# A mixture-of-experts kernel: the 64-row tile of experts 2 to 7 takes the last slots and is worked on behind a test

## The chip, the cores and the metric

The kernel runs on one core of a Trainium2 chip. A core has TensorE (PE in the profile, its weight loads PEld), VectorE (DVE), ScalarE (ACT), GpSimd (POOL) and SyncE (SP), each with its own stream of instructions; a "q" behind a name (PEldq, ACTq) is that engine's sequencer, which handles waits, register loads and branches itself. The metric is the time of one execution in microseconds, the median over runs.

## The reference

A linear attention (a complex-valued decay, 4 batches, 8 heads, 768 steps) gives x with 3072 tokens of 384 numbers. What the change touches is the mixture of experts behind it:

```python
logits = x @ w_gate                                   # 8 experts
noisy_logits = logits + np.log1p(np.exp(x @ w_noise)) * noise
top2 = np.argpartition(-noisy_logits, 2, axis=1)[:, :2]
top2_w = ...                                          # softmax over the two
for e in range(8):
    for k in range(2):
        mask = top2[:, k] == e
        h = np.maximum(x[mask] @ w1[e], 0.0)          # w1[e]: 384 x 1024
        out[mask] += top2_w[mask, k, None] * (h @ w2[e])   # w2[e]: 1024 x 384
```

Each token goes to two of eight experts, so an expert has 768 tokens on average; how many it has is known only when the gates have been computed.

## The kernel before

**Slots.** While the attention runs, each token's row is scattered to a slot of its two experts in a table `xs` in memory. `base_run` counts up by expert: in the end it holds 3072·e plus the tokens of expert e. An expert has room for `CAP` = 832 slots; the slots from `FILL` = 640 on are filled first with empty rows whose token number is out of bounds, so gathers and scatters skip them. If an expert has more than 832 or fewer than 640 tokens (or the decays are extreme), a flag sends the program through a slow path at the end (L856 to L861); in the profiled execution that path is jumped over.

**Tiles.** An expert's 832 slots are worked on in two windows: window 0 has slots 0 to 319 (tiles 0, 1 of 128 rows and tile 2 of 64), window 1 has slots 320 to 831 (tiles 3 to 6). `load_x` brings the rows into `xga` and `xgb`; `x_T` transposes them on PE into `px`, ACT casts them to the high part `x[:, 0]`, DVE subtracts for the low part `x[:, 1]`. `mm1` is the first product, 72 matmuls per window of 320 or 512 columns into `ph`; ACT and DVE make `h` of it. `mm2` is the second product by tile: 24 matmuls of 384 columns for a 128-row tile (L569), 16 for the 64-row tile (L574, L577). DVE multiplies by the gate and adds to the rows `ao[j]` gathered before (`gather_o`, L556), and POOL scatters them to the output (L583). For the 64-row tile ACT copies half of `po` first (L580), and DVE adds twice (L581, L582).

**Order.** Products are made of fp32 numbers split into a high and a low part, which is why each product stands three times. `po` and `px` have two buffers each, `ph` has four. A scheduler puts the instructions of the experts' part in order by priority; the loop over experts writes them as `mm1(e, 0)`, `mm1(e, 1)`, `mm2(e, 0)`, `x_T(e+1, 0)`, `mm2(e, 1)`, `x_T(e+1, 1)`. Weights of the next expert come through three buffers `raw` and are split by ACT (L490) and DVE (L491).

Of the kernel before, what the change touches and what calls it, by code (L numbers as in the profile page):

```python
# [13 lines left out]
I32 = mybir.dt.int32  # L14
AF = mybir.ActivationFunctionType
OP = mybir.AluOpType
# [61 lines left out]
def kernel(  # L78
# [8 lines left out]
    nc = tc.nc  # L87
# [5 lines left out]
    E = w_gate.shape[1]  # L93
# [17 lines left out]
    cp = ctx.enter_context(tc.tile_pool(name="cp", bufs=1))  # L111
# [30 lines left out]
    base_run = cp.tile([128, E], F32, name="base_run")  # L142
# [303 lines left out]

    x3 = xs.rearrange("(e i) r -> e i r", e=E)
    TW = [128, 128, 64, 128, 128, 128, 128]

    def load_x(e, w, dst):  # L450
        if w == 0:
            nc.sync.dma_start(dst[:, 0:2], x3[e, 0:256].rearrange("(p j) r -> p j r", j=2))
            nc.sync.dma_start(dst[0:64, 2], x3[e, 256:320])
        else:
            nc.sync.dma_start(dst, x3[e, 320:CAP].rearrange("(p j) r -> p j r", j=4))

# [11 lines left out]
    def mt(shape, dt, name, **kw):  # L470

        return where.setdefault(name, mpools[-1]).tile(shape, dt, name=name, **kw)
# [38 lines left out]
    def x_T(e, w):  # L511
# [11 lines left out]
        for kk in range(KD):  # L523
            x = XW[w, kk] = mt([128, 2, n], F32R, name=f"x{w}{kk}")
            p = ps_tile("px")
            for j in js:
                o = 128 * (j - js[0])
                gz = nc.tensor.transpose(p[:, o:o + TW[j]], src_t[0:TW[j], j - js[0], kk * 128:(kk + 1) * 128],  # L528
                                    ident[0:TW[j], 0:TW[j]])
                if (e, w) == (0, 1):  # L530
# [22 lines left out]
    def gather_o(e):  # L553
        for j in range(7):
            w = TW[j]
            nc.gpsimd.indirect_dma_start(  # L556
                out=ao[j][0:w, :], out_offset=None, in_=out,
                in_offset=bass.IndirectOffsetOnAxis(ap=OX[e][0:w, j:j + 1], axis=0),
                bounds_check=N - 1, oob_is_err=False)

    def mm2(e, w):
        for j in JS[w]:
            n, o = TW[j], 128 * (j - JS[w][0])
            p = psO.tile([128, 512], F32, name="po")
            a, g = ao[j][0:n, :], GW[e][0:n, j:j + 1]
            if n == 128:
                ms = [(f, i, k2) for f in range(KF) for i, k2 in ((0, 0), (0, 1), (1, 0))]
                for m, (f, i, k2) in enumerate(ms):
                    nc.tensor.matmul(p[:, :DM], HT[w, f][i][:, o:o + 128], W2[f // 2][k2][:, f % 2, :],  # L569
                                     start=(m == 0), stop=(m == len(ms) - 1))  # L570
            else:

                for f in range(KF):
                    nc.tensor.matmul(p[0:2 * n, :DM], HT[w, f][0][:, o:o + 2 * n], W2[f // 2][0][:, f % 2, :],  # L574
                                     start=(f == 0), stop=(f == KF - 1), skip_group_check=True)
                for f in range(KF):
                    nc.tensor.matmul(p[0:n, :DM], HT[w, f][0][:, o:o + n], W2[f // 2][1][:, f % 2, :],  # L577
                                     start=False, stop=(f == KF - 1), skip_group_check=True)
                lo = mt([n, DM], F32, name="lo")
                nc.scalar.copy(lo, p[n:2 * n, :DM])  # L580
                nc.vector.scalar_tensor_tensor(a, lo, g, a, op0=OP.mult, op1=OP.add)  # L581
            nc.vector.scalar_tensor_tensor(a, p[0:n, :DM], g, a, op0=OP.mult, op1=OP.add)  # L582
            nc.gpsimd.indirect_dma_start(  # L583
                out=out, out_offset=bass.IndirectOffsetOnAxis(ap=OX[e][0:n, j:j + 1], axis=0),
                in_=a, in_offset=None, bounds_check=N - 1, oob_is_err=False)
# [34 lines left out]
    for g in range(NG):  # L620
        for lo, hi in ((0, B),) if g < NG - 2 else ((0, B - 1), (B - 1, B)):
            at(B * g + hi + .5 + P["gl"], glog, g, lo, hi)
            at(B * g + hi + .5 + P["gd"], gdis, g, lo, hi)
        if g == NG - 4:
            at(B * g + hi + .5 + P["gd"], load_x, 0, 0, xga)
# [20 lines left out]
    at(NT - .5 - P["q"] + .01, open_pool, qctx)  # L646
    at(P["xt"] + .5, x_T, 0, 0)
    at(P["xt"] + .51, load_x, 1, 0, xga)
    at(P["xu1"] + .5, x_T, 1, 0)
    at(P["w1b"] + .5, load_w1, 1)  # L650
# [30 lines left out]
    for a in ao:  # L681
        nc.vector.memset(a, 0.0)
    load_x(0, 1, xgb)
    mm2(0, 0)
    mm1(1, 0)
    x_T(0, 1)
    load_x(2, 0, xga)
    mm1(0, 1)
    load_x(1, 1, xgb)
    load_w1(2)  # L690
    mm2(0, 1)
    x_T(1, 1)

    lim = mp.tile([128, E], F32, name="lim")
# [3 lines left out]
    nc.vector.tensor_scalar(decm, decm, DEC_MIN, None, op0=OP.is_lt)  # L700
    nc.vector.tensor_reduce(bad[0:112, 0, 1:2], decm[0:112], axis=AX.X, op=OP.max)
    nc.vector.tensor_scalar(bad[:, 1], bad[:, 1], TAN_MAX ** 2, None, op0=OP.is_gt)
    few = mp.tile([128, E], F32, name="few")
    nc.vector.scalar_tensor_tensor(few, lim, float(FILL - CAP), base_run, op0=OP.add, op1=OP.is_gt)
    nc.vector.tensor_tensor(lim, base_run, lim, op=OP.is_gt)
# [14 lines left out]
    for e in range(1, E):  # L720
        load_w2(e)
        gather_o(e)
        if e > 1:
            mm1(e, 0)
            if e + 1 < E:
                load_x(e + 1, 0, xga)
        mm1(e, 1)
        if e + 1 < E:
            load_x(e + 1, 1, xgb)
            if e > 1:  # L730
                load_w1(e + 1)
        mm2(e, 0)
        if e + 1 < E:
            x_T(e + 1, 0)
        mm2(e, 1)
        if e + 1 < E:
            x_T(e + 1, 1)
# [169 lines left out]
```

## Time and profile before

| | |
|---|---|
| median of 3 runs | 731.22 us (730.6 to 732.15) |
| the profiled execution | 730.95 us, of which the span from first to last instruction 729.3 us |
| PE matmul / weight load | 687.4 us (94% of the span) / 609.9 us (84%) |
| DVE / ACT / POOL | 417.6 us (57%) / 329.2 us (45%) / 169.1 us (23%) |
| granted PE clock, mean | 0.992 |

The attention takes about the first 270 us; the rest is the experts, one about every 58 us, with PE hardly ever idle. Busy PE time counts overlapping matmuls as they are modelled, so times between starts are the better measure: eight matmuls of `po` start within 1.39 us.

### The profile page before, as it was taken

Reading aid. Unit: us, or ns where it says so; the run is one execution under the profiler, and the core shown is the slowest. Engines: PE = TensorE matmul, PEld = TensorE weight load, DVE = VectorE, ACT = ScalarE, POOL = GpSimd, SP = SyncE. Lnnn points to the kernel's source line nnn. Section 1 sums busy time; section 2 is a strip of 40 time slices with the busy share of each in tenths; the row PEclk is TensorE's granted clock in tenths of the full one; section 3 lists DMA queues with packets and bytes.
Section 4 is the critical chain, followed back from the end, with each engine's and each line's share of the span. In section 5 each row is a group of like instructions: output and inputs, shape, how many; then the busy total and the mean of one; then the engine's idle time right before and its main releaser. Section 6 shows DMA issues by size and latency. Waiting matters only on the chain.

```text
span 729.3 us, 13448 instructions
## 1 busy us (share of the span) xinstructions
PE 687.4 (94%) x5184; PEld 609.9 (84%) x5184; DVE 417.6 (57%) x946; ACT 329.2 (45%) x545; POOL 169.1 (23%) x187
## 2 busy tenths in 40 slices
PE   1689999999999989999999999999999999999995
PEld 0377687978788979898998998999999899899895
DVE  6788899999988575454264245236227227325321
ACT  6689989897854542423043124124115205203300
POOL 2000002233311263023224124124023123223211
PEclk9989999999999999999999999999999999999998
DMA  7477776844372566145154136028028126212101
GB/s 265 109 246 228 240 211 208 238 140 135 104 221 83 171 208 221 51 133 169 66 191 123 55 123 199 23 88 271 11 66 273 31 74 230 72 37 71 43 28 39
DMA packets 64090, 100.18 MB, mean 137 GB/s; under 512 B 26290, under 2 KB 46363, under 8 KB 64016
## 3 DMA queue, kind: packets, MB, share of 16 engines
q1 hardware_dynamic: 54464, 71.68, 31.9%
q0 software_dynamic: 9552, 27.54, 10.8%
q8 instruction: 43, 0.70, 0.4%
q14 instruction: 31, 0.25, 0.1%
HBM read 68.55 MB, written 32.08 MB: 138 GB/s over the span
## 4 chain that ended last, share of the span: by engine, by line
PE 76%; DVE 9%; ACT 6%; DMA 4%; issue 2%; SPq 1%; POOL 0%; POOLq 0%; DVEq 0%; ACTq 0%
PE ph L545 28%; PE po L569 27%; PE ptr L298 3%; PE psc L307 3%; PE px L528 2%; PE cum L251 2%; DMA raw<-in_moe_w_dram 2%; PE cum L275 2%; PE po L574 2%; PE po L577 2%; PE pY L356 1%; PE psc L545 1%; ACT tr L200 1%; ACT t L200 1%; PE pY L354 1%
## 5 line engine op out<-in xcount | busy, mean ns | idle before, releaser
L569 PE MATMUL po<-w2h,h 128*128 128x384 f32 x768 | 198.8, 336 | 0.0
L545 PE MATMUL ph<-x,w1h 128*128 128x512 f32 (+1 forms) x720 | 194.8, 355 | 0.7 <-DVE h L550 0.5
L545 PEld LDWEIGHTS ph<-x,w1h 128*128 128x128 f32 x720 | 127.8, 188 | 17.0 <-ACT h L547 0.7
L569 PEld LDWEIGHTS po<-w2h,h 128*128 128x128 f32 x768 | 138.9, 188 | 0.9
L569 PE MATMUL po<-w2l,h 128*128 128x384 f32 x384 | 129.0, 336 | 0.0
L545 PE MATMUL ph<-x,w1l 128*128 128x512 f32 (+1 forms) x360 | 127.5, 355 | 0.0
L550 DVE SCALAR_TENSOR_TENSOR h<-ph,h 128x512 fp32r<-128x512 f32 (+2 forms) x176 | 73.3, 453 | 85.3 <-ACT h L547 85.1
L583 POOL DMA_INDIRECT out_dram<-ao,ox x56 | 54.6, 975 | 286.7 <-DVE ao L582 258.0
L547 ACT ACTIVATE h<-ph 128x512 fp32r<-128x512 f32 (+1 forms) x120 | 61.0, 523 | 115.1 <-PE ph L545 100.4
L582 DVE SCALAR_TENSOR_TENSOR ao<-po,gw,ao 128x384 f32<-128x384 f32 (+1 forms) x56 | 34.2, 612 | 121.0 <-PE po L569 120.9
L421 POOL DMA_INDIRECT xs<-xr,sl x48 | 53.8, 1121 | 207.9 <-ACT t L200 103.3
L545 PEld LDWEIGHTS ph<-x,w1l 128*128 128x128 f32 x360 | 67.6, 188 | 7.9
L569 PEld LDWEIGHTS po<-w2l,h 128*128 128x128 f32 x384 | 72.1, 188 | 0.7
L490 ACT CAST w2h<-raw 128x768 fp32r<-128x768 f32 x32 | 26.7, 837 | 91.2 <-PE po L569 87.1
L556 POOL DMA_INDIRECT ao<-out_dram,ox x49 | 54.6, 1113 | 46.2 <-DMA out_dram<-ao,ox 33.4
L307 PE MATMUL psc<-qT,kT 112*128 112x128 f32 x384 | 52.6, 282 | 0.0
L307 PEld LDWEIGHTS psc<-qT,kT 112*128 112x128 f32 x384 | 48.5, 197 | 2.7 <-issue 1.2
L356 PE MATMUL pY<-am,v 128*48 128x128 f32 x384 | 41.4, 275 | 1.2 <-DVE am L308 1.2
L491 DVE TENSOR_TENSOR w2l<-raw,w2h 128x768 fp32r<-128x768 f32 x32 | 30.7, 958 | 13.6 <-ACT w2h L490 12.4
L298 PE MATMUL ptr<-ident,qh 128*112 128x128 f32 x192 | 29.3, 284 | 8.6 <-ACT kT L299 7.9
L580 ACT COPY lo<-po 64x384 f32<-64x384 f32 x8 | 3.8, 477 | 73.4 <-PE po L577 73.3
L491 DVE TENSOR_TENSOR w1l<-raw,w1h 128x1024 fp32r<-128x1024 f32 x24 | 29.2, 1222 | 12.5 <-ACT w1h L490 12.4
(209 smaller groups left out, 981.6 us busy)
## 6 DMA issues: line engine op xcount, KB each, us to landing
raw<-in_moe_w_dram SPq DMA_DIRECT2D x24, 512.0 KB
raw<-in_moe_w_dram SPq DMA_DIRECT2D x32, 384.0 KB
qk<-in_qk_dram SPq DMA_DIRECT2D x24, 384.0 KB
xgb<-xs SPq DMA_DIRECT2D x8, 800.0 KB
re<-in_a_dram SPq DMA_DIRECT2D x12, 384.0 KB
im<-in_a_dram SPq DMA_DIRECT2D x12, 384.0 KB
v<-in_v_dram SPq DMA_DIRECT2D x24, 192.0 KB
out_dram<-zero SPq DMA_DIRECT2D x12, 384.0 KB
```

Of the source, the lines that this page charges most:

```text
L298: nc.tensor.transpose(p[:, h, :], x[:, h, :, :].rearrange("p r x -> p (r x)")[:, 0:112], ident)
L307: nc.tensor.matmul(p[:, j, :], KT[n][:, h, :], QT[n][:, h, :], start=True, stop=True)
L356: nc.tensor.matmul(o, V[n][:, h, :], AM[n][:, h, :], start=not g, stop=True, skip_group_check=True)
L421: d = nc.gpsimd.indirect_dma_start(out=xs, out_offset=bass.IndirectOffsetOnAxis(ap=sl[:, kk, b:b + 1], axis=0), in_=XR[g][:, lo + b, :], i ...
L491: d = nc.vector.tensor_tensor(lo, raw_t, hi.bitcast(F32), op=OP.subtract)
L545: LAST['m'] = nc.tensor.matmul(p[:, :n], W1[e, kk][i][:, f * 128:(f + 1) * 128], XW[w, kk][:, j, :], start=(m == 0), stop=(m == len(ms) - 1))
L547: nc.scalar.activation(h[:, 0:n], p[:, :n], AF.Relu)
L550: LAST['h'] = nc.vector.scalar_tensor_tensor(h[:, dst:dst + b - a], p[:, a:b], 0.0, h[:, a:b].bitcast(F32), op0=OP.max, op1=OP.subtract)
L556: nc.gpsimd.indirect_dma_start(out=ao[j][0:w, :], out_offset=None, in_=out, in_offset=bass.IndirectOffsetOnAxis(ap=OX[e][0:w, j:j + 1], ax ...
L569: nc.tensor.matmul(p[:, :DM], HT[w, f][i][:, o:o + 128], W2[f // 2][k2][:, f % 2, :], start=(m == 0), stop=(m == len(ms) - 1))
L582: nc.vector.scalar_tensor_tensor(a, p[0:n, :DM], g, a, op0=OP.mult, op1=OP.add)
L583: nc.gpsimd.indirect_dma_start(out=out, out_offset=bass.IndirectOffsetOnAxis(ap=OX[e][0:n, j:j + 1], axis=0), in_=a, in_offset=None, bound ...
```

## The change

For experts 2 to 7 tile 2 now holds slots 768 to 831, and window 1 holds slots 256 to 767; experts 0 and 1 keep the old layout. DVE computes `tail`, eight numbers that are 1 where the expert has more than 768 tokens. In `mm2`, tile 2 of experts 2 to 7 stands in an `If`: PE, DVE, ACT and POOL each load the expert's number into a register, compare it and branch. The first product, the gather of `ao[2]` and the transposes of tile 2 are made in any case.

```diff
+    TAILS = range(2, E)
     def load_x(e, w, dst):
         if w == 0:
             nc.sync.dma_start(dst[:, 0:2], x3[e, 0:256].rearrange("(p j) r -> p j r", j=2))
-            nc.sync.dma_start(dst[0:64, 2], x3[e, 256:320])
+            t = CAP - 64 if e in TAILS else 256
+            nc.sync.dma_start(dst[0:64, 2], x3[e, t:t + 64])
         else:
-            nc.sync.dma_start(dst, x3[e, 320:CAP].rearrange("(p j) r -> p j r", j=4))
+            o = 256 if e in TAILS else 320
+            nc.sync.dma_start(dst, x3[e, o:o + 512].rearrange("(p j) r -> p j r", j=4))
...
+    def tail_value(e, engines):
+        return nc.values_load(tail[0:1, e:e + 1], engines=engines, min_val=0, max_val=1,
+                              skip_runtime_bounds_check_because="the result of a comparison")
+
     def mm2(e, w):
         for j in JS[w]:
+            if TW[j] < 128 and e in TAILS:
+                more = tail_value(e, (ENG.PE, ENG.DVE, ENG.Activation, ENG.Pool))
+                with tc.If(more > 0):
+                    mm2_tile(e, w, (j,))
+            else:
+                mm2_tile(e, w, (j,))
+
+    def mm2_tile(e, w, js):
+        for j in js:
...
+    tail = cp.tile([1, E], I32, name="tail")
+    nc.vector.scalar_tensor_tensor(tail, lim[0:1], -64.0, base_run[0:1], op0=OP.add, op1=OP.is_lt)
```

An `If` is scheduled as one piece, and that moves other work. On PE, behind the second tile of expert 2 (the names: `po` second product, `px` transposes of expert 3's rows, `ph` expert 3's first product), there stood before:

```order
L569 MATMUL po<-w2h_4602,h_4725 128x384
L574 MATMUL po<-w2h_4584,h_4627 128x384 [waits DVE_49]
...
L577 MATMUL po<-w2l_4603,h_4725 64x384
L528 MATMUL px<-ident,xga 128x128 [waits DMAHW2_49,PE_49]
...
L569 MATMUL po<-w2h_4584,h_4741 128x384 [waits DVE_49,Activation_49]
...
L528 MATMUL px<-ident,xga 128x128 [waits DVE_49]
```

and now there stands:

```order
L586 MATMUL po<-w2h_4604,h_4727 128x384
L532 MATMUL px<-ident,xga 128x128 [waits DMAHW2_49,PE_49]
...
L549 MATMUL ph<-x_4959,w1h_4850 128x320 [waits DVE_49,Activation_49]
...
L532 MATMUL px<-ident,xgb 128x128 [waits DMAHW7_49,DVE_49]
...
L566 TENSOR_LOAD tail [waits DVE_49]
L573 COMPARE_AND_BRANCH
L591 MATMUL po<-w2h_4586,h_4629 128x384
...
L594 MATMUL po<-w2l_4605,h_4727 64x384
L573 UNCONDITIONAL_BRANCH
L573 UNCONDITIONAL_BRANCH [waits PE_49]
L586 MATMUL po<-w2h_4586,h_4743 128x384
```

Ahead of the branch now stand 16 transposes (9 of window 0, 7 of the 12 of window 1) and 8 matmuls of the next expert's first product; before, six transposes followed tile 2 directly, three stood among the matmuls of tile 3, and the 12 of window 1 came after tile 6. The 16 matmuls of tile 2 lie between the two branches. Who skips them lands on the second unconditional branch, at which PE waits for its own count (`PE_49`), that is until every matmul ahead of it has ended.

On DVE, at the same place (`ao` sums of the tiles, `x` the low parts of expert 3's rows), there stood first:

```order
L582 SCALAR_TENSOR_TENSOR ao_3658<-po,gw,ao_3658 128x384 [waits DMASW6_49,PE_49]
L581 SCALAR_TENSOR_TENSOR ao_3659<-lo,gw,ao_3659 64x384 [waits DMASW7_49,Activation_49]
L533 TENSOR_TENSOR x_4950<-px,x_4950 128x320 [waits Activation_49]
L582 SCALAR_TENSOR_TENSOR ao_3659<-po,gw,ao_3659 64x384 [waits DVE_49]
L533 TENSOR_TENSOR x_4957<-px,x_4957 128x320 [waits Activation_49]
L533 TENSOR_TENSOR x_4964<-px,x_4964 128x320 [waits Activation_49]
L582 SCALAR_TENSOR_TENSOR ao_3660<-po,gw,ao_3660 128x384 [waits DMASW0_49,PE_49]
```

and now:

```order
L599 SCALAR_TENSOR_TENSOR ao_3658<-po,gw,ao_3658 128x384 [waits DMASW6_49,PE_49]
L537 TENSOR_TENSOR x_4959<-px,x_4959 128x320 [waits Activation_49]
...
L537 TENSOR_TENSOR x_5098<-px,x_5098 128x512 [waits Activation_49]
L566 TENSOR_LOAD tail [waits DVE_49]
L573 COMPARE_AND_BRANCH
L598 SCALAR_TENSOR_TENSOR ao_3659<-lo,gw,ao_3659 64x384 [waits DMASW7_49,Activation_49]
L599 SCALAR_TENSOR_TENSOR ao_3659<-po,gw,ao_3659 64x384 [waits DVE_49,PE_49]
L573 UNCONDITIONAL_BRANCH
L573 UNCONDITIONAL_BRANCH [waits DVE_49]
L599 SCALAR_TENSOR_TENSOR ao_3660<-po,gw,ao_3660 128x384 [waits DMASW0_49,PE_49]
```

All four `x` differences that PE waits for now stand ahead of DVE's branch. For expert 7, which has no next expert, PE's branch follows the second tile directly:

```order
L586 MATMUL po<-w2h_7294,h_7417 128x384
L566 TENSOR_LOAD tail
L573 COMPARE_AND_BRANCH
L591 MATMUL po<-w2h_7276,h_7319 128x384 [waits DVE_49]
...
L594 MATMUL po<-w2l_7295,h_7417 64x384
L573 UNCONDITIONAL_BRANCH
L573 UNCONDITIONAL_BRANCH [waits PE_49]
L586 MATMUL po<-w2h_7276,h_7431 128x384 [waits DVE_49,Activation_49]
```

There the first matmul of tile 3 also waits for DVE, which has to empty the buffer of tile 1.

## Rows read from the trace of the kernel before

**Rows 1.** Chain that ended last, share by line (the page's part 4).

```profile
PE 76%; DVE 9%; ACT 6%; DMA 4%; issue 2%; SPq 1%; POOL 0%; POOLq 0%; DVEq 0%; ACTq 0%
```

**Rows 2.** Stretches: us, busy of PE, PEld, DVE, ACT, POOL, clock, DMA share, GB/s.

```profile
413.38:472.08 58.70, 58.23 (x327) 53.81 (x325) 24.79 (x49) 17.26 (x30) 15.57 (x14) 1.00 0.36 117
472.08:530.47 58.39, 58.39 (x327) 53.88 (x325) 24.88 (x49) 17.41 (x30) 14.68 (x14) 1.00 0.36 119
```

**Rows 3.** Whom PE waited for from 354.98 to 704.96 us.

```profile
PE ph L545 <- DVE h L550: 0.5, 1, 0.5
```

**Rows 4.** The chain in order of time: start us, us, what.

```profile
469.30 1.39 PE po L574 x8
470.69 1.39 PE po L577 x8
472.08 0.99 PE px L528 x6
...
702.19 1.39 PE po L574 x8
703.58 1.39 PE po L577 x8
```

**Rows 5.** POOL's DMA queue, experts 2 to 7 in turn: packets, MB, share.

```profile
q0 software_dynamic: 864, 2.38, 12.3%
q0 software_dynamic: 864, 2.33, 11.4%
q0 software_dynamic: 864, 2.47, 11.8%
q0 software_dynamic: 864, 2.34, 12.2%
q0 software_dynamic: 864, 2.32, 12.5%
q0 software_dynamic: 864, 2.25, 12.3%
```

**Rows 6.** Line 856, PE's register load: ns min/median/max, start us.

```profile
L856 PEldq TENSOR_LOAD <-flag x1: 496/496/496, 718.3 to 718.3; - x1
```

**Rows 7.** Instructions of each engine from 718.34 us to PE's end.

```profile
718.34:721.70 3.36, 3.27 (x19) 2.95 (x17) 0.05 (x1) 0.00 (x0) 0.97 (x1) 1.00 0.15 52
```

**Rows 8.** Line 858, the branch over the slow path, by engine.

```profile
L858 ACTq COMPARE_BRANCH  x1: 50/50/50, 705.9 to 705.9; - x1
L858 ACTq EVENT_SEMAPHORE  x1: 17/17/17, 708.4 to 708.4; - x1
L858 PEldq COMPARE_BRANCH  x1: 3617/3617/3617, 719.4 to 719.4; - x1
L858 PEldq EVENT_SEMAPHORE  x1: 51/51/51, 723.0 to 723.0; - x1
L858 POOLq COMPARE_BRANCH  x1: 45/45/45, 723.2 to 723.2; - x1
```

**Rows 9.** Line 903, POOL's next instruction behind that branch.

```profile
L903 POOLq DRAIN  x3: 45/107/4671, 723.7 to 729.0; - x3
```

**Rows 10.** DMA of instruction blocks for PE from 719.4 to 723.1 us.

```profile
q8 instruction: 1, 0.02, 1.5%
```

**Rows 11.** Timeline around one tile 2: start us, us, engine, line, what.

```profile
410.27 0.33 PE L569 MATMUL po<-w2h,h 128*128 128x384 f32 x1
410.64 0.62 DVE L582 SCALAR_TENSOR_TENSOR ao<-po,gw,ao 128x384 f32<-128x384 f32 x1 [3.54 <-PE po L569]
...
414.10 0.27 PE L528 MATMUL px<-ident,xga 64*128 64x64 f32 x1
414.30 0.19 PEld L569 LDWEIGHTS po<-w2h,h 128*128 128x128 f32 x1
...
415.63 0.58 PE L528 MATMUL px<-ident,xga 128*128 128x128 f32 x3
416.25 0.43 ACT L532 CAST x<-px 128x320 fp32r<-128x320 f32 x1 [1.41 <-PE px L528]
416.71 0.49 DVE L533 TENSOR_TENSOR x<-px,x 128x320 fp32r<-128x320 f32 x1 [0.85 <-ACT x L532]
```

**Rows 12.** The chain where expert 3's first product waits for weights.

```profile
431.68 5.80 DMA raw<-in_moe_w_dram
437.50 1.06 ACT w1h L490
438.58 1.23 DVE w1l L491
```

More of the change, by code (lines that the diff above doesn't have):

```diff
@@ L448 @@
     TW = [128, 128, 64, 128, 128, 128, 128]
+    TAILS = range(2, E)
+    ENG = mybir.EngineType
     def load_x(e, w, dst):
```

## The prediction

> **What bounds the kernel now.** I began with the chain that ended last: 76% of it is PE, and no other engine has a tenth [rows 1]. A share is an average, so I then cut the experts' part into periods of one expert. In two of them PE is busy 58.23 of 58.70 us and 58.39 of 58.39 us, at a granted clock of 1.00, that is 2.4 GHz, while DVE, ACT and POOL have 25, 17 and 15 us, and DMA a share of 0.36 [rows 2]. The list of waits says the same: over 350 us PE waited once for another engine, for 0.5 us [rows 3]. The reader should see that here a matmul less is its time less, and that work taken from another engine is worth nothing by itself. The chain in order of time gives the price of what can be skipped: the two halves of tile 2 take 1.39 us each, with transposes right behind them [rows 4], so 2.78 us per expert.
>
> **Who skips.** The profile doesn't print the token counts, but POOL's DMA queue moves each token's row of 384 fp32 numbers (1536 bytes) twice per expert, gathered and scattered, and leaves empty slots out. 768 tokens would be 2 x 768 x 1536 bytes = 2.36 MB. Experts 2 to 7 moved 2.38, 2.33, 2.47, 2.34, 2.32 and 2.25 MB [rows 5], or about 775, 758, 804, 762, 755 and 732 tokens. So experts 2 and 4 run tile 2, and 3, 5, 6 and 7 skip it: gross 4 x 2.78 = 11.1 us of PE. The copy, two sums and scatter that ACT, DVE and POOL skip lie beside PE's 58 us: nothing.
>
> **Load and compare.** A register load on PE's sequencer took 0.496 us [rows 6] and a compare where nothing was far away 0.045 to 0.05 us [rows 8]. Six experts pay 0.55 us each if PE's array stands still meanwhile, 3.3 us in all; nothing if the sequencer is ahead. It is ahead: when it began that load at 718.3 us, the array still had 19 matmuls and 17 weight loads before it [rows 7]. The order shows 24 matmuls between tile 1 and the load (16 transposes, 8 of the first product), so the 17 nearest, at 0.165 us or a little less (six transposes in 0.99 us [rows 4]), keep the array busy for some 2.5 us, and the load ends about 2 us before the array runs dry. That cover is gone only if the sequencer itself is held by a wait shortly before the load; the last that could are transposes waiting for DVE to free `px`. I take 0 (bounds 0 and 0.55), also for experts 2 and 4. On DVE, ACT and POOL the same instructions delay only sums, casts and scatters that PE needs microseconds later.
>
> **The bubble of a skip.** Who skips lands on a jump that waits for PE's own count, so the array must drain. From the start of the last transpose: 0.27 its own time, 0.04 until a semaphore is seen (410.27 + 0.33 to 410.64), 0.19 for the next weights [rows 11]; 0.05 for the waiting instruction; and about 0.20 for the jump, since POOL went from its compare at 723.2 to the DRAIN at 723.7 through two jumps in some 0.45 us [rows 8, 9]. Sum 0.75, less the 0.165 that a next matmul would have come later anyway: 0.59. Experts 3, 5 and 6 thus save 2.78 - 0.59 = 2.2 us each (bounds of the bubble 0.3, without jump and wait, and 0.9: savings 2.5 to 1.9).
>
> Expert 7 has nothing between tile 1 and the branch, and tile 3 needs the `po` buffer of tile 1, which tile 2 used to give DVE time to empty. Now: 0.33 last matmul, 0.04, 0.62 DVE's sum, 0.04, 0.05, 0.19 = 1.27, less 0.17 = 1.10 (the jump passes beside the sum). It saves 1.7 us (bounds 1.5 to 1.9).
>
> **Work that moves.** Transposes and 8 first-product matmuls of the next expert now stand ahead of the branch, and tile 3 behind it. PE has the same work in another order, so it costs only where it waits. A transposed tile goes through ACT and DVE: from three transposes starting at 415.63 to DVE's end at 417.20, 1.57 us [rows 11]. Three such tiles follow each other through two `px` buffers, with window 1's transposes and the 8 matmuls to fill in; laying these rows end to end I get 0.1 to 0.2 us of waiting, about as much as the old order lost around its own transposes (58.70 less 58.23 in one period, 0 in the next [rows 2]). I take 0; five boundaries at 0.3 either way give plus or minus 1.5. DVE's `tail`, one operation on eight numbers, lies beside PE's work: 0. The other slots in tile 2 and window 1 change what is loaded, not how much.
>
> **Sum.** 3 x 2.2 + 1.7 = 8.3 us. The profiled execution took 730.95, so 722.7; the median of the runs is 0.27 above that execution: 722.9, forecast **723.0**. With the bounds above (skips plus or minus 1.1, moved work 1.5, loads up to 1.1 on the taken two) its own range is 720.0 to 725.3.
>
> **Rivals.** *The load is exposed.* If the sequencer's lead is used up by waits for `px`, all six pay 0.55, and the compare and jump come on top of the drain, some 0.2 more: 4 x 0.75 + 2 x 1.1 = 5.2 us back, so 728. Against it: the lead of 17 to 19 matmuls [rows 7].
>
> *Each skip fetches instructions, partly covered.* PE's branch over the slow path took 3617 ns, ACT's next instruction came 2.45 us after its branch, and POOL's branch took 45 ns [rows 8]; during PE's a 16 KB block of instructions came for PE [rows 10]. So a branch can cost more than tile 2 itself. That one jumped over some 700 of PE's instructions; the new one jumps over 33 (16 weight loads, 16 matmuls and a jump), whereas POOL's, over about 95, cost nothing. I therefore take no fetch as likely. If each skip fetched and 17 queued matmuls covered 2.5 of its 0.5 + 3.62, the array would stand about 1.5 us longer per skip, and the taken ones lose a little: 5 us back, 728.
>
> *The same, not covered: slower.* If the branch stalls the sequencer with the array dry, a skip costs 0.50 + 3.62 + 0.64 (drain and load) = 4.8 us against 2.78 won: 2.0 x 4 = 8 us lost, 739. It decides from the point where the bubble of a skip exceeds 2.78 us. For it speaks only PE's one row of 3617 ns; against it the short jump and the lead.
>
> The Trainium skill has a rule that speaks for these two ("Runtime: NRT & Kernel Launch", section "Instruction fetch mechanics"): instructions come in blocks of 16 KiB, 256 instructions, and a taken branch whose target lies outside the two blocks at hand must wait for a fetch, one reason why it calls runtime control flow expensive. The trace agrees with the size of the block [rows 10] and with a hit on POOL and a miss on PE [rows 8]; by the same rule a target 33 instructions ahead lies in the block at hand or the next, and the sum stays 723, where its warning taken alone would give 728 or 739.
>
> *PE no longer waits for nothing.* The first product now begins about 8 matmuls, 1.2 us, earlier against the old order, and its weights arrive when they did: the one place where it already waited was raw weights at 437.48, then ACT 1.06 and DVE 1.23 us to split them [rows 12]. If each of five experts waits 0.8 us there, 4 us are given back: 727. Against it: only 0.5 us of such waits in 350 us [rows 3], and DMA at a share of 0.36.
>
> *The change skips nothing* (the counts from [rows 5] or the test are off, or what is skipped comes back as waits elsewhere): 731.
>
> **How the numbers follow.** Forecast 0.64; load exposed 0.09; fetch partly covered 0.07; weights late 0.08; no gain 0.05; fetch not covered 0.07. A change of 0.2%, 1.5 us, is about what a measurement of this kernel can tell from none: so faster 0.64 + 0.09 + 0.07 + 0.08 = 0.88, same 0.05, slower 0.07. The range reaches from 720.0 over the cases around 727 and 728, to 728.5; outside stand the last two cases, 0.12, and the tails of the forecast.
>
> **What the next profile would show.** Right: four periods of an expert (3, 5, 6, 7) with 16 matmuls fewer on PE, no rows of tile 2's lines in them, and a gap of 0.6 us before tile 3's first matmul, 1.1 in expert 7; in experts 2 and 4 no gap ahead of tile 2, and PE's TENSOR_LOAD rows that end before the array's last transpose starts. PE's compare rows near 50 ns, with no instruction block fetched beside them. The other engines' branches may wait as long as they like, if PE's waits do not name them. Wrong: compares or landing jumps of microseconds (fetch); gaps of 0.5 to 1 us also in experts 2 and 4 (load); waits of the first product for DVE's or ACT's weights, or of transposes for DVE, at each boundary (moved work).

## The result, and the profile after

The changed kernel takes 723.9 us (median of 4 runs, 722.71 to 724.25) against 730.91 us (4 runs, 729.47 to 732.15): a ratio of 0.9903, 95% interval 0.9886 to 0.992. That is 1.0% faster; 723.0 was forecast, and 720.0 to 728.5 as the range. The profiled execution took 722.71 us, where the sum had given 722.7.

The first view to read is that of stretches, from each expert's first second-product matmul to the next expert's (for expert 7 to the end); it answers to [rows 2]. Columns: us, then busy time and count of PE, PEld, DVE, ACT and POOL, granted clock, DMA share, GB/s.

```profile
402.77:461.19 58.42, 58.34 (x326) 53.88 (x325) 25.20 (x49) 17.37 (x30) 14.26 (x14) 1.00 0.36 118
461.19:517.18 55.99, 55.84 (x310) 51.39 (x309) 23.95 (x47) 16.89 (x29) 13.32 (x13) 1.00 0.38 124
517.18:575.25 58.07, 58.07 (x326) 53.80 (x325) 25.16 (x49) 17.37 (x30) 15.39 (x14) 1.00 0.37 119
575.25:631.32 56.07, 55.92 (x310) 51.38 (x309) 23.93 (x47) 16.89 (x29) 13.23 (x13) 1.00 0.38 122
631.32:687.49 56.17, 55.55 (x311) 51.39 (x309) 20.41 (x40) 14.27 (x26) 12.91 (x13) 1.00 0.16 49
687.49:720.96 33.47, 25.39 (x145) 24.78 (x143) 4.39 (x7) 0.60 (x1) 5.92 (x6) 0.93 0.10 36
```

Experts 3, 5, 6 and 7 have 16 matmuls fewer on PE and two operations fewer on DVE; 2 and 4 have all of theirs. These are the four that the gathered bytes [rows 5] had named. The matmuls that are left still run at a clock of 1.00; the last stretch has 0.93 as it had before, since PE stands idle at its end.

The list of waits of PE from 400 us on, which answers to [rows 3]:

```profile
PE po L586 <- DVEq L573: 0.8, 1, 0.8
PE ph L549 <- DVE h L554: 0.4, 1, 0.4
PE po L586 <- PEq L573: 0.2, 1, 0.2
```

Of the six branches it names two, those of experts 7 and 6. The others are shorter than what it lists, and have to be read from starts. The wait in the middle is not at a branch: it is one of the first product in expert 6's stretch, of which more below. Around expert 3's skip the timeline of PE and of the weight loads shows:

```profile
472.87 0.31 PE L549 MATMUL ph<-x,w1l 128*128 128x320 f32 x1
473.01 0.49 PE L532 MATMUL px<-ident,xgb 128*128 128x128 f32 x3
473.62 0.19 PEld L586 LDWEIGHTS po<-w2h,h 128*128 128x128 f32 x1 [0.36 <-issue]
473.65 0.41 PE L586 MATMUL po<-w2h,h 128*128 128x384 f32 x1
473.90 0.34 PE L586 MATMUL po<-w2l,h 128*128 128x384 f32 x1
```

The instructions of the load's and the branch's lines there (ns min/median/max, first and last start):

```profile
L566 PEldq TENSOR_LOAD <-tail x1: 308/308/308, 472.8 to 472.8; - x1
L573 PEldq COMPARE_BRANCH  x1: 221/221/221, 473.3 to 473.3; - x1
L573 PEldq EVENT_SEMAPHORE  x1: 51/51/51, 473.5 to 473.5; - x1
```

And DVE's timeline just ahead:

```profile
472.30 0.49 DVE L537 TENSOR_TENSOR x<-px,x 128x320 fp32r<-128x320 f32 x1 [0.61 <-ACT x L536]
```

The three transposes start at 473.01, 473.12 and 473.23, the last ends at 473.50, and tile 3's first matmul starts at 473.65: 0.42 from start to start, where 0.11 is the distance between transposes, so 0.31. The second matmul comes after 0.25 in place of 0.17, another 0.08. The skip cost 0.4 us, where 0.59 was forecast. The load began at 472.8, when four matmuls were left: not 17. The last three of these, the transposes, stand ahead of the load in PE's stream and wait for DVE to free `px`; its subtraction ended at 472.79, and the load began 0.06 us later.

Expert 7, all engines:

```profile
695.66 0.34 PE L586 MATMUL po<-w2h,h 128*128 128x384 f32 x1
696.03 0.62 DVE L599 SCALAR_TENSOR_TENSOR ao<-po,gw,ao 128x384 f32<-128x384 f32 x1 [3.55 <-PE po L586]
696.77 0.19 PEld L586 LDWEIGHTS po<-w2h,h 128*128 128x128 f32 x1 [1.09 <-issue]
696.80 0.41 PE L586 MATMUL po<-w2h,h 128*128 128x384 f32 x1 [0.80 <-DVEq L573]
```

As forecast, what ends the gap is tile 1's sum: 1.14 from start to start, less 0.17, and 0.08 at the second matmul, together 1.05 (forecast 1.10). The wait is put down to DVE's branch (`DVEq L573`), which stands directly behind that sum in DVE's stream; the duration to look at is the sum's 0.62. (In e6_twoloads, an experiment below, DVE's branch comes only when tile 3 has begun, and the distance of 1.14 is the same.)

Expert 2, which takes the body, PE and PEld, and its register load:

```profile
414.59 0.49 PE L532 MATMUL px<-ident,xgb 128*128 128x128 f32 x3
415.15 0.99 PEld L591 LDWEIGHTS po<-w2h,h 128*128 128x128 f32 x6 [0.31 <-issue]
415.16 1.14 PE L591 MATMUL po<-w2h,h 128*128 128x384 f32 x5
```

```profile
L566 PEldq TENSOR_LOAD <-tail x1: 488/488/488, 414.4 to 414.4; - x1
```

The last transpose starts at 414.81, tile 2 at 415.16: 0.35 where 0.11 is usual. So a taken branch was not free. The load ended at 414.9, when the last transpose had already started.

The chain that ended last can't be compared with [rows 1]: it now leads back over POOL's scatters and register loads alone, and names no PE. This program with branches is better read by stretches.

### The profile page after: what moved, and what is told of

Its sections match the earlier page's. It is cut to its first block, busy times and chain, and to the rows that moved or that the text cites. A ratio compares the mean times of both kernels' runs of the same rounds, so it can differ in the third digit from the quotient of the medians.

```text
span 721.0 us, 13355 instructions
## 1 busy us (share of the span) xinstructions
PE 678.2 (94%) x5120; PEld 600.7 (83%) x5120; DVE 414.1 (57%) x939; ACT 326.9 (45%) x541; POOL 163.6 (23%) x183
## 5 line engine op out<-in xcount | busy, mean ns | idle before, releaser
L549 PE MATMUL ph<-x,w1h 128*128 128x512 f32 (+1 forms) x720 | 197.1, 357 | 0.7 <-DVE h L554 0.4
L600 POOL DMA_INDIRECT out_dram<-ao,ox x52 | 51.0, 980 | 278.5 <-DVE ao L599 259.2
L599 DVE SCALAR_TENSOR_TENSOR ao<-po,gw,ao 128x384 f32<-128x384 f32 (+1 forms) x52 | 31.8, 613 | 129.4 <-PE po L586 129.2
L494 ACT CAST w2h<-raw 128x768 fp32r<-128x768 f32 x32 | 26.6, 836 | 100.1 <-PE po L586 95.4
L560 POOL DMA_INDIRECT ao<-out_dram,ox x49 | 52.3, 1066 | 52.6 <-DMA out_dram<-ao,ox 31.9
L536 ACT CAST x<-px 128x512 fp32r<-128x512 f32 (+1 forms) x42 | 21.0, 519 | 52.2 <-PE px L532 51.4
L298 PEld LDWEIGHTS ptr<-ident,qh 128*112 128x112 f32 x192 | 22.5, 139 | 17.2 <-ACT kT L299 9.2
```

Source lines behind the costliest of these rows:

```text
L298: nc.tensor.transpose(p[:, h, :], x[:, h, :, :].rearrange("p r x -> p (r x)")[:, 0:112], ident)
L549: LAST['m'] = nc.tensor.matmul(p[:, :n], W1[e, kk][i][:, f * 128:(f + 1) * 128], XW[w, kk][:, j, :], start=(m == 0), stop=(m == len(ms) - 1))
L560: nc.gpsimd.indirect_dma_start(out=ao[j][0:w, :], out_offset=None, in_=out, in_offset=bass.IndirectOffsetOnAxis(ap=OX[e][0:w, j:j + 1], ax ...
L600: nc.gpsimd.indirect_dma_start(out=out, out_offset=bass.IndirectOffsetOnAxis(ap=OX[e][0:n, j:j + 1], axis=0), in_=a, in_offset=None, bound ...
```

## The experiments

**How they are read.** Runs of whole kernels differ by some 0.2%, which is what is asked about here, so beside the ratios each experiment is read from its trace, by the stretches used above: us from an expert's first second-product matmul to the next one's, expert 7 to the end.

| kernel | e2 | e3 | e4 | e5 | e6 | e7 | sum | ratio to before (95%) |
|---|---|---|---|---|---|---|---|---|
| before | 58.71 | 58.39 | 58.10 | 58.39 | 58.00 | 35.52 | 327.11 | 1 |
| the change | 58.42 | 55.99 | 58.07 | 56.07 | 56.17 | 33.47 | 318.19 | 0.9903 (0.9886 to 0.992) |
| e1_layout | 57.99 | 58.40 | 58.02 | 58.40 | 58.01 | 35.60 | 326.42 | 0.9991 (0.9981 to 1.0002) |
| e2_static | 57.99 | 56.08 | 58.01 | 55.60 | 55.23 | 33.06 | 315.97 | 0.9842 (0.9822 to 0.9863) |
| e3_always | 58.51 | 58.87 | 58.35 | 58.59 | 58.17 | 35.70 | 328.19 | 1.004 (1.0024 to 1.0056) |
| e4_never | 55.77 | 56.24 | 55.69 | 56.25 | 55.67 | 34.32 | 313.94 | 0.9824 (0.9803 to 0.9845) |
| e6_twoloads | 58.26 | 56.08 | 58.33 | 56.35 | 55.74 | 34.03 | 318.79 | 0.9916 (0.9899 to 0.9934) |
| e8_far | 61.26 | 61.04 | 58.90 | 61.11 | 60.29 | 34.37 | 336.97 | 1.0212 (1.0194 to 1.0231) |
| e9_after (the change again) | 58.66 | 56.00 | 58.03 | 55.97 | 55.59 | 34.08 | 318.33 | 0.9903 (0.9882 to 0.9924) |

Two parts vary by themselves: what lies before expert 2's matmul differs by up to 3 us among kernels that do the same there (it begins at 401.19 in e9_after, at 404.38 in e3_always), and what follows PE's last matmul in expert 7 by up to 1 us. Up to that matmul, expert 7 is much steadier: 27.59 us in before and e1_layout, 25.86 in the change and in e9_after, 24.81 in e2_static. And e5_first, e6_twoloads and e8_far ran together on another chip, on which the kernel before took 740.61 us; their stretches compare, their times only as ratios.

**The slots alone (e1_layout).** No test; every expert works on tile 2.

```diff
-            if TW[j] < 128 and e in TAILS:
-                more = tail_value(e, (ENG.PE, ENG.DVE, ENG.Activation, ENG.Pool))
-                with tc.If(more > 0):
-                    mm2_tile(e, w, (j,))
-            else:
-                mm2_tile(e, w, (j,))
+            mm2_tile(e, w, (j,))
```

> The slots of the changed kernel without any test: tile 2 of all experts is worked on. Theory (the gain is PE's skipped matmuls and nothing else): no difference from before, 730.9 us within 0.7. Rival 'layout' (other slots in tile 2 and window 1 arrive at other times or cost something else): a difference of more than 1 us, either way.

730.68 us against 730.6 for before in the same runs. The other slots cost nothing, and this kernel is the one to measure tests against. Its stretches:

```profile
403.30:461.29 57.99, 57.99 (x326) 53.82 (x325) 24.78 (x49) 17.33 (x30) 14.94 (x14) 1.00 0.36 118
461.29:519.69 58.40, 58.40 (x326) 53.90 (x325) 24.89 (x49) 17.48 (x30) 14.43 (x14) 1.00 0.36 119
...
694.12:729.72 35.60, 27.93 (x161) 27.29 (x159) 5.62 (x9) 1.08 (x2) 6.83 (x7) 0.95 0.10 34
```

**Tile 2 left out by the program (e2_static).**

```diff
+            if TW[j] == 128 or e in (0, 1, 2, 4):
+                mm2_tile(e, w, (j,))
```

> The slots of the changed kernel, and tile 2's second product, sums and scatter of experts 3, 5, 6 and 7 are left out when the program is written, with no test; 2 and 4 work on theirs. Theory: the gross 4 x 2.78 = 11.1 us, so 719.8, which leaves some 3 us (8.2 of 11.1 in the profiles) as the price of finding out at run time: gaps of 0.3 us in 3, 5, 6, 1.0 in 7, about 0.25 in 2 and 4, the rest noise between executions. Rival 'moved work' (the new order, not the branches, costs the difference): the order here is the old one, so it gives 719.8 as well, but the always-taken version then loses as much as 3 us. Rival 'the gain is not worth its count' (work skipped comes back as waits for weights or DVE): 722 or more.

719.79 us, as the theory had it (719.8). So nearly all of the 11.1 us gross is there: PE was the bound and stays it, and little behind it takes the gain back. By stretches the gain is 10.45. Experts 5 and 6 got 2.80 and 2.78, expert 7 got 2.78 up to its last matmul; expert 3 got only 2.32, the rest went into the first product in its stretch, whose 144 matmuls took 0.46 us longer from start to start.

**Everyone takes the body (e3_always), no one does (e4_never).** One number each, in the comparison that makes `tail`: the first added line is e3_always, the second e4_never.

```diff
-    nc.vector.scalar_tensor_tensor(tail, lim[0:1], -64.0, base_run[0:1], op0=OP.add, op1=OP.is_lt)
+    nc.vector.scalar_tensor_tensor(tail, lim[0:1], -832.0, base_run[0:1], op0=OP.add, op1=OP.is_lt)
+    nc.vector.scalar_tensor_tensor(tail, lim[0:1], 3072.0, base_run[0:1], op0=OP.add, op1=OP.is_lt)
```

> The changed kernel with the comparison set so that every expert takes the body: nothing is skipped, all loads, compares and branches are there, and the moved order too. Theory: six times about 0.25 us of gap at the branch (the start of tile 2's first matmul 0.35 after the last transpose where 0.11 is usual), so 731.0 to 733.0 us. Rival 'load exposed': six times 0.75 or more, 735 or over. Rival 'moved work': 733 to 735 with gaps elsewhere than at the branch.

734.32 us, above the theory's 731 to 733 and short of the 735 of the exposed load. The profiled execution took 2.8 us more than that of e1_layout. In the stretches, the machinery with nothing skipped costs 328.19 - 326.42 = 1.8 us for six experts; the other 1.1 us lie before expert 2, in the part that varies by itself, and are not explained here. The branch itself is 0.24 us in expert 2 and 0.04 to 0.07 in 3 to 6 (starts of last transpose and first matmul of tile 2, less 0.11), with 0.1 more among the first matmuls behind it. In expert 7, where the 24 matmuls of tile 1 stand directly ahead of the test, there is no gap. The rest is in the first product: by their starts its matmuls took 0.3 to 0.6 us longer per stretch than in e1_layout, while those of the second product took 0.1 to 0.2 less. Neither theory fits alone: there is some of each.

> The changed kernel with the comparison set so that no expert takes the body; the rows of experts 2 and 4 beyond 768 are left out of the sum. Theory: experts 2 and 4 save 2.78 - 0.3 + 0.25 (their taken branch goes) = 2.7 us each, so 5.4 less than the changed kernel, 718.0 to 719.0. Rival 'fetch' (a jump over the body can cost microseconds in some places): some of the six gaps are over 1 us, and the gain is under 4.

718.25 us, inside the theory's band; no gap is over 1 us but that of expert 7. Expert 2's gap is the longest of the transposes' five, and its load, the first of its kind, the slowest:

```profile
414.38 0.49 PE L532 MATMUL px<-ident,xgb 128*128 128x128 f32 x3
415.21 0.41 PE L586 MATMUL po<-w2h,h 128*128 128x384 f32 x1 [0.33 <-PEq L573]
```

```profile
L566 PEldq TENSOR_LOAD <-tail x1: 488/488/488, 414.2 to 414.2; - x1
```

0.61 from the last transpose (414.60) to tile 3, where the change's expert 3 with a load of 308 ns had 0.42. A load that is 0.18 longer makes a gap that is 0.19 longer, in the same place of the program. In experts 2 to 6 the load has no time to spare.

**The load doubled (e6_twoloads).**

```diff
                 more = tail_value(e, (ENG.PE, ENG.DVE, ENG.Activation, ENG.Pool))
+                more = more + tail_value(e, (ENG.PE, ENG.DVE, ENG.Activation, ENG.Pool))
```

> The changed kernel with the load doubled on each engine: the value is read twice and the two are added before the comparison. Theory (in experts 2 to 6 the load starts only about 4 matmuls, 0.65 us, before the array runs dry, because the sequencer has just waited for DVE; load and compare, 0.31 + 0.22, just fit): the second load and the addition no longer fit, some 0.3 to 0.5 us more in five experts, nothing in expert 7, where 17 matmuls stand ahead: 1.5 to 2.5 us more than the changed kernel, 725.4 to 726.4, and gaps of 0.7 to 0.9 us from start to start at the skips. Rival 'as predicted, 17 matmuls ahead everywhere': no change, 723.9.

A miss in size: 0.9916 against 0.9903, and 318.79 us in the stretches against 318.19 and 318.33. The scheduler put the last three transposes behind the branch, so the wait for DVE that used to stand before the load was gone. The load now began behind an earlier one of DVE's subtractions (it ended at 480.44), with seven matmuls to go:

```profile
L566 PEldq TENSOR_LOAD <-tail x2: 304/447/590, 480.5 to 480.9; - x2
```

```profile
481.33 0.45 PE L549 MATMUL ph<-x,w1h 128*128 128x320 f32 x2
482.11 0.41 PE L587 MATMUL po<-w2h,h 128*128 128x384 f32 x1 [0.32 <-PEq L574]
```

The gap is 482.11 - 481.48 - 0.15 = 0.48 us, 0.17 over the single load's 0.31, where 0.3 to 0.5 were expected over it. So it was not a clean doubling; that the cover of the load is bounded is better seen in expert 2 above. In expert 7, where 17 matmuls stood ahead, the second load cost nothing, as expected: 1.14 us from start to start, as with one.

**Tile 2 first (e5_first, e10_first: the same kernel twice).**

```diff
-        for j in JS[w]:
+        for j in sorted(JS[w], key=lambda j: TW[j]) if e in TAILS else JS[w]:
             if TW[j] < 128 and e in TAILS:
```

> Tile 2 of experts 2 to 7 is written ahead of tiles 0 and 1 instead of behind them, test and all. The scheduler then puts PE's load and branch among the matmuls of window 1's first product, with no transpose ahead of it, and in expert 7 tile 1's sum no longer stands behind a skip. Theory (the price of a test is the drain, plus what the wait of the last transposes for DVE leaves of the load uncovered): gaps of about 0.4 us at all four skips, expert 7's among them, none to speak of in 2 and 4, so the static version's 719.8 + 4 x 0.4 = 721.4, 720.8 to 722.5. Rival 'a test costs the same wherever it stands': 723.9, as the changed kernel.

> The changed kernel again, as the measure for the next one on the same chip: 0.990 of before, 0.9885 to 0.992.

> Tile 2 written first, again, beside the changed kernel on the same chip. Theory (by the gaps of both traces, the experts' part is 1.6 us shorter): 0.9880 of before, 0.0015 to 0.003 below the changed kernel. Rival 'same price wherever it stands': no difference.

e5_first has a ratio of 0.9895 (0.9875 to 0.9915), 8.2 us under before by the medians where 8.4 to 10.1 were expected. On one chip, 721.92 us and 0.9884 (0.9861 to 0.9906) for e10_first, against 722.68 us and 0.9903 (0.9882 to 0.9924) for the change. The ratio is 0.0019 lower, where 0.0015 to 0.003 was expected, but the intervals overlap: by the times it is not decided that this version is faster. In the trace its tests are cheaper. The stretches of e10_first (tile 2 of an expert now lies at the end of the stretch of the expert before it):

```profile
405.41:460.94 55.53, 55.38 (x311) 51.21 (x309) 23.92 (x47) 17.11 (x30) 13.41 (x13) 1.00 0.37 124
460.94:519.42 58.48, 58.48 (x326) 53.99 (x326) 23.93 (x47) 16.88 (x29) 13.43 (x13) 1.00 0.35 119
519.42:574.92 55.50, 55.35 (x310) 51.17 (x310) 24.97 (x49) 17.50 (x31) 14.89 (x14) 1.00 0.37 125
574.92:630.96 56.04, 55.89 (x309) 51.31 (x310) 23.93 (x47) 16.89 (x30) 13.12 (x13) 1.00 0.37 123
630.96:686.56 55.60, 55.45 (x310) 51.27 (x310) 20.51 (x40) 14.39 (x27) 12.92 (x13) 1.00 0.16 50
```

The compare of expert 3, and PE's timeline there:

```profile
L573 PEldq COMPARE_BRANCH  x1: 221/221/221, 457.0 to 457.0; - x1
```

```profile
460.40 0.39 PE L549 MATMUL ph<-x,w1l 128*128 128x512 f32 x1
460.94 0.41 PE L586 MATMUL po<-w2h,h 128*128 128x384 f32 x1
```

The compare is done 3 us before the array runs dry, so here the load had the cover of 17 matmuls that the prediction counted on, and the gap is the bare drain: 0.54 less the usual 0.23, again 0.31. Against the slots alone less 2.77 the four skips (experts 3, 5, 6, 7) cost 0.31, 0.25, 0.41 and 0.36 us, the one taken (expert 4) 0.08: 1.4 us in all. Expert 2's test lies ahead of these stretches; there tile 2's first matmul starts 0.23 us after the one ahead of it (387.04 to 387.27), which is the usual distance, so it shows no gap. In e9_after the same reckoning gives 0.67, 0.37, 0.01, 0.34 and 0.35 for experts 2 to 6, and expert 7 still has its gap of 1.05: 2.8 us. What the version saves is the wait for tile 1's sum (1.05 down to 0.36) and the taken branch of expert 2; a plain skip costs the same 0.3 to 0.4 in either place, so the theory's reason holds for the first half only.

**The skipped body made long (e8_far, e11_mid64, e12_mid128).** No one takes it, as in e4_never; only the distance of the jump on PE changes: `FAR` is 47 for 384 matmuls, 7 for 64, 15 for 128.

```diff
-                for f in range(KF):
+                for f in list(range(KF)) * (FAR if e in TAILS else 1):
                     nc.tensor.matmul(p[0:2 * n, :DM], HT[w, f][0][:, o:o + 2 * n], W2[f // 2][0][:, f % 2, :],
```

> The version that skips all six tiles (its comparison never holds, rows of experts 2 and 4 beyond 768 left out), with the skipped body on PE made long: 384 matmuls in place of 16, so the jump goes over some 768 instructions in place of 33. Nothing of the body runs. Theory (a branch on PE costs microseconds only when its target has to be fetched, and 33 instructions ahead it has not): compare rows of 2.4 to 3.6 us in place of 0.2, with instruction blocks fetched beside them, 2 to 3.5 us more per expert in 2 to 6 and about 0.5 in 7, 728 to 736 against 718.25. Rival 'distance does not matter, the 3.6 us of the branch over the slow path had another reason': 718.

> All six tiles skipped, the skipped body on PE 64 matmuls long in place of 16 (a jump over 129 instructions). Theory (only a target that has to be fetched costs microseconds, and a block that came in is 256 instructions): compare rows near 0.2 us in most of the six, at most one or two of 2 us or more; span near the 716.5 of the short body. Rival 'every jump on PE beyond some tens of instructions fetches': six rows over 2 us.

> The same with a body of 128 matmuls (a jump over 257 instructions, about one block). Theory: some of the six compares near 0.2 us, some over 2 us, by where the blocks begin. Rival 'distance beyond some tens': all six over 2 us; rival 'PE keeps more than two blocks': none.

PE's branch rows of e4_never (33 instructions), e11_mid64 (129), e12_mid128 (257) and e8_far (769), in this order, one fence each:

```profile
L573 PEldq COMPARE_BRANCH  x6: 202/204/228, 414.8 to 687.8; - x6
```

```profile
L574 PEldq COMPARE_BRANCH  x6: 207/316/353, 416.2 to 691.9; - x6
```

```profile
L574 PEldq COMPARE_BRANCH  x6: 318/342/1757, 414.7 to 691.9; - x6
```

```profile
L574 PEldq COMPARE_BRANCH  x6: 3487/3710/4217, 423.8 to 719.8; - x6
```

In e12_mid128 two of the six took 1.28 and 1.76 us, where some over 2 were expected, four 0.32 to 0.35. The two long rows are those of a block of instructions that was still coming in. The first is expert 3's; in the 1.15 us ahead of it, from 469.80 to 470.95, the instruction queue began one block:

```profile
L574 PEldq COMPARE_BRANCH  x1: 1281/1281/1281, 471.0 to 471.0; - x1
```

```profile
q8 instruction: 1, 0.02, 5.7%
```

Expert 5's jump at 584.22 is the same: a block began at 583.07. These rows ended 2.4 and 2.9 us after their block began, those of e8_far 2.3 to 2.7 us after theirs, which began only behind the compare. None of the other four had a block under way. Two cases are few, but a block under way is not enough by itself: in the change, one was coming in at expert 6's skip (from 642.46 on), and the row took 0.22 us. Why the rows of e11_mid64 are mostly 0.1 us longer than those of e4_never is open.

The two of middle length had one execution each, 722.39 and 721.86 us, above what was expected of the first (a span near 716.5, and it was 720.7); beside the branch, some of their first products wait more than in e4_never. In e8_far each branch took more than tile 2 itself, and its ratio is 1.0212: with the same skips the kernel is slower than before. That is 3.9% over e4_never, some 28 us, where 10 to 18 were expected: each row is longer than thought, and the clock fell behind it (last section). Its profiled execution was the fastest of six; there the stretches are 23.0 us longer than e4_never's, of which 18 are longer gaps at the branches. Around expert 3's jump, PE's timeline and the DMA queues from 484.88 to 488.6 us:

```profile
484.64 0.49 PE L533 MATMUL px<-ident,xgb 128*128 128x128 f32 x3
488.74 0.41 PE L587 MATMUL po<-w2h,h 128*128 128x384 f32 x1 [3.61 <-PEq L574]
```

```profile
q8 instruction: 1, 0.02, 1.6%
```

A block of instructions comes in while PE stands, as at the slow path before [rows 10]. In the change's skip (472.8 to 473.7 us) the instruction queue moved nothing.

In expert 7 the same jump, a row of 3.73 us from 719.84 on, cost almost nothing, because the 17 matmuls ahead of it and DVE's sum went on meanwhile:

```profile
722.33 0.34 PE L587 MATMUL po<-w2h,h 128*128 128x384 f32 x1
723.89 0.41 PE L587 MATMUL po<-w2h,h 128*128 128x384 f32 x1 [1.22 <-PEq L574]
```

That is 1.56 us from start to start against 1.14 in e4_never and in the change.

## Why the prediction was right, point by point

**What bounds the kernel, and who skips**: right. The static version gave the gross gain, and the four experts are those read from the bytes.

**The sum.** Against e1_layout's stretches the change moved experts 2 to 7 by +0.43, -2.41, +0.05, -2.33, -1.84 and -2.13 us, -8.2 in all; the prediction had 0, -2.2, 0, -2.2, -2.2 and -1.7, -8.3. So close a total hides terms that erred in both directions, and that the profiled execution met the sum to 0.01 us is luck. Expert 7 is the best example: up to its last matmul it gained 1.73 us, as forecast, and 0.40 lies behind that matmul, in the part that varies by itself. What the tests cost is less well known than the gain: e2_static is shorter than the change by 2.2 us in the stretches, by 0.6% or some 4.5 us in the ratios.

Three smaller sums of the prediction do not come out, and the forecast hangs on none of them: its own bounds add up to 720.3 to 726.6, not 720.0 to 725.3; in the partly covered fetch 4 x 1.5 is 6, not 5; and the exposed load counts 1.1 for each taken expert, twice its 0.55.

**The bubble of a skip**: the mechanism was right, the size too large, 0.4 for 0.59. Two terms failed. The 0.20 for the jump is not in the gap: compare and jump are one row of 0.22 us (not the 0.05 forecast for the compare) and are over at 473.48, before the last transpose ends at 473.50. And the 0.19 for the next weights came to little: tile 3's first matmul starts 0.03 after its weight load (473.62, 473.65). What is left is the drain, 0.04 until the count is seen, 0.05 for the waiting instruction, some 0.06 until the matmul starts, and 0.08 for the second matmul, which the prediction didn't have.

**The load lies hidden under 17 matmuls**: wrong in experts 2 to 6, right in 7, where it began at 692.7 with 17 matmuls to go. The row it came from [rows 7] was taken in a stretch without waits. Here the last transposes wait for DVE directly ahead of the load, the case that the prediction named and set to 0. In e6_twoloads, which has another order there, the load again began behind a subtraction of DVE. Four matmuls, 0.63 us, remained, against 0.31 + 0.22 for load and compare, which just fit; the first load, 0.49, did not, and expert 2 paid 0.24 at the branch. That is the price of the step; expert 4's load fitted, and its branch cost 0.04. Both paid 0.1 more at tile 2's second matmul (0.27 from start to start, where 0.17 is usual), as did e3_always, and why is open.

**Moved work**: 0 forecast, within its bound of 1.5. By their starts, and against e1_layout, the new order saves some 0.2 us per stretch among the matmuls of the second product and loses 0.2 to 0.3 in the first product, 0.7 in expert 6's stretch; why, is not shown but for expert 6. There one matmul waited for DVE's `h`, the 0.4 in the list of waits. In e9_after, the same kernel, that wait is not there, and expert 6's stretch gained 2.42 instead of 1.84: much of this varies from one execution to the next. The kernel before had such a wait too, in expert 2's stretch:

```profile
440.42 0.53 PE L545 MATMUL ph<-x,w1h 128*128 128x320 f32 x2 [0.47 <-DVE h L550]
```

This is the 0.47 us (58.70 less 58.23 [rows 2]) that the prediction put down to the old order's transposes; it is the one wait of [rows 3]. e3_always puts branch and moved work together at 1.8 us for six experts.

**The rival of the fetch** did not happen, but it is real. Its point of decision, a bubble over 2.78 us, was passed in e8_far by distance alone: 0.2 us over 33 instructions, 3.5 to 4.2 over 769. The Trainium skill's rule ("Runtime: NRT & Kernel Launch", section "Instruction fetch mechanics": a taken branch waits for a fetch when its target is outside the two blocks of 256 instructions at hand) agrees with these rows: none of the jumps over 33 or 129 instructions waited for a block, all those over 769 did. The two slow jumps over 257 waited for a block that had been asked for before the jump. The partly covered fetch of the prediction is real too: in e8_far's expert 7 all but 0.4 us of the row was covered.

**The other rivals**: the load exposed, true in expert 2 alone, as above; the first product's waits, a small part, as above, and that weights are their cause is not shown; no gain, refuted.

## What to carry to other kernels

On an engine that is the bound, a runtime skip is worth its matmuls less the drain of the array, here 2.8 less 0.4 us, if the jump is short; the same skip over 769 instructions lost more than it saved where the engine stood still meanwhile. Put the test where its engine's queue is long and no wait stands directly ahead of it, and where the next work doesn't need a buffer that the skipped work was giving time to; e10_first shows both in its trace, though not yet in its times. To read it, cut the trace into stretches between marks that both kernels have, against a variant with the data layout but without the test; the list of waits names too little of it.

## What was not expected of the hardware

After a long stall the granted clock fell, though not at once. In e8_far the stretches around expert 3's jump read:

```profile
484.90:488.70 3.80, 0.23 (x3) 0.00 (x0) 0.66 (x1) 0.00 (x0) 0.00 (x0) 1.00 0.32 110
488.70:489.90 1.20, 1.16 (x7) 1.19 (x8) 0.00 (x0) 0.00 (x0) 0.00 (x0) 0.99 0.06 14
489.90:493.50 3.60, 3.60 (x13) 3.60 (x12) 0.00 (x0) 0.00 (x0) 0.00 (x0) 0.53 0.00 0
493.50:497.00 3.50, 3.50 (x23) 3.50 (x22) 0.62 (x1) 0.00 (x0) 0.97 (x1) 1.00 0.00 0
```

PE idles for 3.6 us, runs 1.2 us at full clock, then 3.6 us at 0.53, about the lower level of 1.2 GHz, 13 matmuls where 21 would have fitted, and then is back at 2.4. The same happened in experts 2, 5 and 6, where PE ran 0.3, 0.4 and 1.2 us at full clock first. It cost some 1.6 us each time on top of the stall (the second product's matmuls took 26.6 us per expert from start to start, 25.1 in e4_never); after expert 4's jump, as long a stall, the clock stayed at 1.00. The change's own gaps of 0.3 to 1.1 us never did this.
